# mLSTM attention and two MoE layers on one core: the last 64 input rows in another split, one pass for the weights' low part

## The chip, the core and the metric

The kernel runs on one core of one Trainium2 chip. The metric is the device time of one execution in microseconds (us), lower is better. TensorE (PE) multiplies 128x128 tiles, loads of its stationary operand (PEld) overlap with it; VectorE (DVE), ScalarE (ACT) and GpSimd (POOL) do elementwise work; SyncE (SP) issues every DMA. Each engine has its own queue of instructions, written out once, and works it off in order; semaphores order the engines among each other.

## The reference

```python
# attention: batch 2, 8 heads, 768 steps, head size 40
m_new = max(f + m, i);  f_stab = exp(f + m - m_new);  i_stab = exp(i - m_new)
C = f_stab * C + i_stab * outer(v, k);   n = f_stab * n + i_stab * k
y[t] = sigmoid(o) * (C @ q) / max(abs(n @ q), 1)
# x: (1536 tokens, 320), the heads side by side
def moe(x):   h = x @ w_in;  return (h - tanh(h)) @ w_out          # 320 -> 2048 -> 320
def moe2(x):  h = x @ w_in;  return (h * tanh(softplus(h))) @ w_out
out = moe2(moe(attention))                                        # weights are float64
```

## The kernel before

**Layout.** Tokens are cut into 12 pieces of 128: piece j holds chunk c = j // 2 of batch b = j % 2. Attention runs in chunks of 128 steps with a carried state `C`. Layer 0 (the first MoE) takes six blocks of two pieces, layer 1 three blocks of four. The 2048 hidden columns are 16 tiles f of 128; for each f the host lays the 128 columns of `w_in` (rows 0 to 127, 128 to 255, 320 columns of `w_out`, and the last 64 rows twice, one copy on each half of the partitions) side by side: 704 columns (`WC`) of float64, which arrive as pairs of 32-bit words.

**High and low parts.** TensorE multiplies a rounded float32 form. Each operand is kept as a high part (rounded by ACT) and a low part (the rest, from a subtraction), and a product is summed from high times high, high times low and low times high. `conv_w` makes a weight tile `w` from a `raw` tile: three passes over the raw words (L202 and L214 on DVE, L210 on ACT; for layer 1 also L204 on DVE, and L207 in place of L210), the high copy of 704 columns (L217, ACT), the low part of the first 576 columns (L220, DVE), and the low part of the upper 64 partitions of the last 128 columns, which overwrites the high part there (L221, DVE). For f = 0 of layer 0, L220 and L221 run on POOL. So the last weight piece (`PCH`) holds high over low.

`transpose_x` transposes a token piece by three PE transposes (`xt`, L288; the last 64 columns of x are doubled beforehand by a copy of ACT, L428), ACT copies the high part of all three pieces (L290) and DVE subtracts the low part of all three in one pass (L293). `mm1` (L576 on, matmul L586, tile `h`) does eight matmuls per f and block: HI0 and HI1 with x high, HI0 and HI1 with x low, LO0 and LO1 with x high, and `PCH` with the last x piece high and low.

**The rest of a tile.** `tile1` (L595 to L617) makes g from h on ACT (tanh twice, square, relu with bias) and DVE (two tensor operations, a predicated copy), ACT rounds it to `gh` (L597), POOL subtracts `gl` (L598); `mm2` (L649 to L651) multiplies by `w_out` into `acc`. `attention(j)` runs `nb` (PE, L358 from chunk 1 on), `Dm` (ACT exp, L361, then POOL's AFFINE_SELECT, L363), `dl` and `wv` (POOL), `sc` (PE) and DVE's product with `Dm` (L389), `it` and `pv` (PE), `hv`, `den` and `xo` (DVE, L401 to L423), then the transpose and the state update `st` (PE, L310).

**Order.** The program is recorded with attention, conversion of weights and layer 0 interleaved by tables of steps (`CUT`, `ahead`, `conv_to`), and a list scheduler that simulates durations sets the final order of each engine's queue. While the first eight weight tiles are converted, filler matmuls (`w_ps`, L690) stand in PE's queue. Between the tiles f = 4 to 7 of the first block, ACT loads another table, takes the sigmoid of the output gates for chunks 1 to 5 (L264) and loads the first table back.

**Slots.** Weight tiles have 16 slots, which the gate tiles (`n_all`, `n0`, `gi`, ...) hold first. The first four raw tiles lie in slots of the pool `xp` that later hold transposed x; the rest in three slots of `rawp`. `nr` (the gate rows that DMAs spread into `md` and `sd`) has a place of its own.

Of the kernel before, what the change touches and what calls it, by code (L numbers as in the profile page):

```python
# [8 lines left out]
F32 = mybir.dt.float32  # L9
F32R = mybir.dt.float32r  # L10
# [15 lines left out]
def kernel(  # L26
# [21 lines left out]
    REM0, REM1 = 256 + DM, 256 + DM + 128  # L48
    HI0, HI1, OUT_HI, PCH = 0, 128, 256, REM0
    LO0, LO1, OUT_LO = WC, WC + 128, WC + 256  # L50
    WT = WC + 256 + DM
# [64 lines left out]
    nr = once.tile([P, S - EC * L], F32R, name="nr")  # L116
# [57 lines left out]
    def load_w(n=1):  # L174
        for _ in range(n):
            if pending_loads:
                layer, f = pending_loads.pop(0)
                early = layer == 0 and f < ER
                t = (xp if early else rawp).tile(
                    [P, 2 * WC], U32, tag="x" if early else "raw", name="raw", bufs=NB - 1 if early else None  # L180
                )
                queued(
                    lambda: nc.sync.dma_start(out=t, in_=(w1, w2)[layer][f].bitcast(U32)), layer == 0 and f < CUT[0]
                )
                raw[layer, f] = t
# [3 lines left out]
    def conv_w(layer, f, first=(), behind=()):  # L189
# [29 lines left out]
        with after(scored[NP + 1] if (layer, f) == (0, CUT[0] - 1) else []):  # L219
            eng.tensor_tensor(w[:, WC:WT], in0=zf[:, 0:REM0], in1=wf[:, 0:REM0], op=ALU.subtract)  # L220
        lows[layer, f] = eng.tensor_tensor(w[64:P, REM0:REM1], in0=zf[64:P, REM0:REM1], in1=wf[64:P, REM0:REM1], op=ALU.subtract)  # L221
# [55 lines left out]
    def new_xT(layer, bi):  # L277
        nt = len(blk[layer, bi]) * L
        p, m = (late.get("x", xp), M1) if layer == 0 else (x2pool(bi), M2)
        t = p.tile([P, 2, 3, m], F32R, tag="x", name="xT", bufs=len(supers[0]) if layer else 1 if p is not xp else NB - 1)  # L280
        xT[layer, bi] = tuple(t[:, n, :, 0:nt] for n in range(2))

    def transpose_x(layer, bi, pos):
# [5 lines left out]
        hi, lo = (t[:, :, pos * L:(pos + 1) * L] for t in xT[layer, bi])  # L289
        chain[:] = [x, nc.scalar.activation(out=hi, in_=t_ps, func=AF.Copy)]  # L290

        def low():
            chain.append(nc.vector.tensor_tensor(lo, in0=t_ps, in1=hi.bitcast(F32), op=ALU.subtract))  # L293
# [281 lines left out]
    def mm1(i):  # L575
        l, bi, fs, nt = span(i)  # L576
        t = ps_h.tile([P, MX], F32, tag="h", name="h")[:, 0:len(fs) * nt]
        xh, xl = xT[l, bi]
        pairs = [
            (HI0, xh, 0), (HI1, xh, 1), (HI0, xl, 0), (HI1, xl, 1), (LO0, xh, 0), (LO1, xh, 1), (PCH, xh, 2), (PCH, xl, 2),  # L580
        ]
        for k, f in enumerate(fs):
            w = wtile[l, f]
            for n, (o, x, kk) in enumerate(pairs):
# [396 lines left out]
```

## Time and profile before

| what | value |
|---|---|
| median of 3 runs | 448.72 us (448.59 to 448.79) |
| the profiled execution | 447.9 us, of which its span 446.2 us |
| PE busy | 436.4 us (98%), 3114 matmuls |
| PEld busy | 399.5 us (90%) |
| DVE busy | 305.4 us (68%), 521 instructions |
| ACT busy | 283.5 us (64%), 519 instructions |
| POOL busy | 99.2 us (22%), 107 instructions |
| mean granted TensorE clock | 0.999 |

The span runs from the first to the last instruction; 1.7 us of the execution lie outside it. Matmuls are pipelined and each one's end is modelled, so PE's busy share counts time in which it is not at its peak, and the filler matmuls count as busy too. The share of DVE is a mean over stages: it is nearly full in the first 160 us and below a quarter in the last 86.

### The profile page before, as it was taken

Reading aid. Unit: us, or ns where it says so; the run is one execution under the profiler, and the core shown is the slowest. Engines: PE = TensorE matmul, PEld = TensorE weight load, DVE = VectorE, ACT = ScalarE, POOL = GpSimd, SP = SyncE. Lnnn points to the kernel's source line nnn. Section 1 sums busy time; section 2 is a strip of 40 time slices with the busy share of each in tenths; the row PEclk is TensorE's granted clock in tenths of the full one; section 3 lists DMA queues with packets and bytes.
Section 4 is the critical chain, followed back from the end, with each engine's and each line's share of the span. In section 5 each row is a group of like instructions: output and inputs, shape, how many; then the busy total and the mean of one; then the engine's idle time right before and its main releaser. Section 6 shows DMA issues by size and latency. Waiting matters only on the chain.

```text
span 446.2 us, 7979 instructions
## 1 busy us (share of the span) xinstructions
PE 436.4 (98%) x3114; PEld 399.5 (90%) x3114; DVE 305.4 (68%) x521; ACT 283.5 (64%) x519; POOL 99.2 (22%) x107
## 2 busy tenths in 40 slices
PE   9899989999999999999999999999999999999996
PEld 5657979899899999999999999999999888999996
DVE  7899999978899896578999987898522211211112
ACT  6687987485786858889889877666434322333331
POOL 2307235343452521333333331000000000000000
PEclk9999999999999999999999999999999999999999
DMA  8986526423244210002222110543010000100001
GB/s 247 368 301 206 187 62 226 125 70 95 62 151 136 66 67 0 1 2 66 65 67 66 65 66 0 195 132 128 0 60 0 1 1 1 42 18 0 1 0 59
DMA packets 22728, 38.03 MB, mean 85 GB/s; under 512 B 1348, under 2 KB 17028, under 8 KB 22692
## 3 DMA queue, kind: packets, MB, share of 16 engines
q1 hardware_dynamic: 22692, 37.54, 25.7%
q8 instruction: 24, 0.39, 0.4%
q14 instruction: 12, 0.10, 0.1%
HBM read 35.41 MB, written 1.97 MB: 84 GB/s over the span
## 4 chain that ended last, share of the span: by engine, by line
PE 86%; DVE 8%; ACT 4%; issue 1%; ACTq 0%; DVEq 0%
PE h L586 37%; PE acc L649 12%; PE acc L651 12%; PE acc L650 12%; PE pv L409 3%; PE sc L385 2%; PE w_ps L690 2%; PE it L396 2%; PE xt L288 2%; DVE g L613 1%; DVE t L614 1%; DVE g L617 1%; DVE Dm L389 1%; ACT raw L210 1%; PE nb L358 1%
## 5 line engine op out<-in xcount | busy, mean ns | idle before, releaser
L586 PE MATMUL h<-xT,w 128*128 128x256 f32 (+1 forms) x1152 | 205.8, 321 | 0.5 <-DVE w L220 0.2
L586 PEld LDWEIGHTS h<-xT,w 128*128 128x128 f32 x1152 | 168.7, 188 | 15.7 <-issue 0.9
L649 PE MATMUL acc<-w,gh 128*128 128x320 f32 x384 | 119.5, 312 | 0.6 <-ACT gh L597 0.4
L650 PE MATMUL acc<-w,gh 128*128 128x320 f32 x384 | 118.8, 310 | 0.0
L651 PE MATMUL acc<-w,gl 128*128 128x320 f32 x384 | 114.0, 310 | 0.0
L598 POOL TENSOR_TENSOR gl<-g,gh 128x512 fp32r<-128x512 f32 x48 | 62.5, 1303 | 139.1 <-ACT gh L597 134.1
L630 DVE TENSOR_TENSOR gl<-g,gh 128x512 fp32r<-128x512 f32 x48 | 33.2, 691 | 87.4 <-ACT g L629 87.2
L628 ACT ACTIVATE gh<-h 128x512 fp32r<-128x512 f32 x48 | 28.7, 598 | 78.1 <-PE h L586 78.0
L649 PEld LDWEIGHTS acc<-w,gh 128*128 128x128 f32 x384 | 72.2, 188 | 3.4 <-ACT gh L597 0.7
L650 PEld LDWEIGHTS acc<-w,gh 128*128 128x128 f32 x384 | 72.2, 188 | 2.4
L651 PEld LDWEIGHTS acc<-w,gl 128*128 128x128 f32 x384 | 70.4, 188 | 0.7 <-issue 0.4
L617 DVE COPY_PREDICATED g<-u,t 128x512 f32<-128x512 uint32 x48 | 39.3, 824 | 10.0 <-ACT u L615 9.6
L597 ACT ACTIVATE gh<-g 128x512 fp32r<-128x512 f32 x48 | 30.3, 632 | 22.8 <-DVE g L617 21.5
L613 DVE TENSOR_TENSOR g<-u,h 128x512 f32<-128x512 f32 x48 | 32.7, 680 | 13.8 <-ACT u L610 3.9
L615 ACT ACTIVATE u<-u,bias 128x512 f32<-128x512 f32 x48 | 34.8, 725 | 8.2 <-DVE g L613 8.2
L217 ACT ACTIVATE w<-raw 128x704 fp32r<-128x704 f32 x32 | 27.2, 861 | 10.8 <-DVE raw L214 10.5
L614 DVE TENSOR_TENSOR t<-h,t 128x512 f32<-128x512 f32 x48 | 32.8, 684 | 0.0
L214 DVE SCALAR_TENSOR_TENSOR raw<-raw 128x704 uint32<-128x704 uint32 x32 | 32.0, 1007 | 1.0 <-ACT raw L207 0.4
L220 DVE TENSOR_TENSOR w<-raw,w 128x576 fp32r<-128x576 f32 x31 | 29.1, 939 | 1.9 <-ACT w L217 1.8
L610 ACT ACTIVATE u<-u 128x512 f32<-128x512 f32 x48 | 30.4, 636 | 0.0
L608 ACT ACTIVATE u<-h 128x512 f32<-128x512 f32 x48 | 28.1, 585 | 1.3 <-PE h L586 1.3
L629 ACT ACTIVATE g<-h 128x512 f32<-128x512 f32 x48 | 28.5, 594 | 0.0
(108 smaller groups left out, 445.0 us busy)
## 6 DMA issues: line engine op xcount, KB each, us to landing
raw<-in_w_dram SPq DMA_DIRECT2D x32, 704.0 KB
qk_t<-in_qk_dram SPq DMA_DIRECT2D x12, 512.0 KB
kv_t<-in_kv_dram SPq DMA_DIRECT2D x12, 324.0 KB
out_dram<-xo SPq DMA_DIRECT2D x12, 160.0 KB
xo<-in_og_dram SPq DMA_DIRECT2D x2, 800.0 KB
xo<-in_og_dram SPq DMA_DIRECT2D x1, 320.0 KB
sd<-nr SPq DMA_DIRECT2D x20, 4.0 KB
md<-nr SPq DMA_DIRECT2D x10, 8.0 KB
```

The lines of the kernel that those rows point to most:

```text
L214: third[layer, f] = nc.vector.scalar_tensor_tensor(z, in0=z, scalar=3, in1=lo32, op0=ALU.logical_shift_left, op1=ALU.bitwise_or)
L586: y = nc.tensor.matmul(t[:, k * nt:(k + 1) * nt], lhsT=w[:, o:o + P], rhs=x[:, kk, :], start=(n == 0), stop=(n == len(pairs) - 1),)
L598: nc.gpsimd.tensor_tensor(gl, in0=g, in1=gh.bitcast(F32), op=ALU.subtract)
L610: squared[:] = [nc.scalar.activation(out=u, in_=u, func=AF.Square, scale=G_SA)]
L613: mark[:] = [nc.vector.tensor_tensor(g, in0=u, in1=h, op=ALU.mult)]
L614: nc.vector.tensor_tensor(t, in0=h, in1=t, op=ALU.subtract)
L615: relus[i] = nc.scalar.activation(out=u, in_=u, func=AF.Relu, bias=bias[:, 0:1])
L617: chosen[i] = nc.vector.copy_predicated(out=g, mask=u.bitcast(U32), data=t)
L630: mark.append(nc.vector.tensor_tensor(gl, in0=g, in1=gh.bitcast(F32), op=ALU.subtract))
L649: turn(lambda: nc.tensor.matmul(a, lhsT=gh[:, sl], rhs=wh, start=(f in ends_), stop=False))
L650: turn(lambda: nc.tensor.matmul(a, lhsT=gh[:, sl], rhs=wl, start=False, stop=False))
L651: turn(lambda: nc.tensor.matmul(a, lhsT=gl[:, sl], rhs=wh, start=False, stop=end))
```

## The change

The weight tile grows from 1280 to 1408 columns: both halves of the last piece keep the high part (`PCH`), and its low part lies behind the other low parts (`PCL`), on both halves. So one subtraction over 704 columns replaces the two passes of 576 and of 64x128. On the other side, the x tile has five pieces instead of six: pieces 0 to 2 are the high parts, where the upper half of piece 2 is overwritten by its low part (L292, 64x128), and pieces 3 and 4 are the low parts of the first two (L294, 128x256). `mm1` still does eight matmuls, in another order: the third is now `PCH` with piece 2, the last `PCL` with piece 2. The first four raw tiles now lie in slots of the weight tiles, and `nr` in a slot of `xp`.

```diff
--- before.py
+++ after.py
@@ -45,10 +45,9 @@
     NF, _, WC = w1.shape
     D1 = D + 1
     HP = P // 2
-    REM0, REM1 = 256 + DM, 256 + DM + 128
-    HI0, HI1, OUT_HI, PCH = 0, 128, 256, REM0
-    LO0, LO1, OUT_LO = WC, WC + 128, WC + 256
-    WT = WC + 256 + DM
+    HI0, HI1, OUT_HI, PCH = 0, 128, 256, 256 + DM
+    LO0, LO1, OUT_LO, PCL = WC, WC + 128, WC + 256, WC + 256 + DM
+    WT = 2 * WC
 
     BLOCKS = [2, 2, 2, 2, 2, 2]
     SUPER = [[4], [4], [4]]
@@ -113,7 +112,7 @@
     uT = once.tile([P, NCH, BH], F32, name="uT")
 
     EC = 1
-    nr = once.tile([P, S - EC * L], F32R, name="nr")
+    nr = xp.tile([P, S - EC * L], F32R, tag="x", name="nr", bufs=NB - 1)
 
 
 
@@ -176,9 +175,7 @@
             if pending_loads:
                 layer, f = pending_loads.pop(0)
                 early = layer == 0 and f < ER
-                t = (xp if early else rawp).tile(
-                    [P, 2 * WC], U32, tag="x" if early else "raw", name="raw", bufs=NB - 1 if early else None
-                )
+                t = (wp if early else rawp).tile([P, 2 * WC], U32, tag="w" if early else "raw", name="raw")
                 queued(
                     lambda: nc.sync.dma_start(out=t, in_=(w1, w2)[layer][f].bitcast(U32)), layer == 0 and f < CUT[0]
                 )
@@ -217,8 +214,7 @@
         cvd[:] = [nc.scalar.activation(out=w[:, 0:WC], in_=zf, func=AF.Copy)]
         eng = nc.gpsimd if (layer, f) == (0, 0) else nc.vector
         with after(scored[NP + 1] if (layer, f) == (0, CUT[0] - 1) else []):
-            eng.tensor_tensor(w[:, WC:WT], in0=zf[:, 0:REM0], in1=wf[:, 0:REM0], op=ALU.subtract)
-        lows[layer, f] = eng.tensor_tensor(w[64:P, REM0:REM1], in0=zf[64:P, REM0:REM1], in1=wf[64:P, REM0:REM1], op=ALU.subtract)
+            lows[layer, f] = eng.tensor_tensor(w[:, WC:WT], in0=zf, in1=wf[:, 0:WC], op=ALU.subtract)
         wtile[layer, f] = w
 
 
@@ -277,8 +273,10 @@
     def new_xT(layer, bi):
         nt = len(blk[layer, bi]) * L
         p, m = (late.get("x", xp), M1) if layer == 0 else (x2pool(bi), M2)
-        t = p.tile([P, 2, 3, m], F32R, tag="x", name="xT", bufs=len(supers[0]) if layer else 1 if p is not xp else NB - 1)
-        xT[layer, bi] = tuple(t[:, n, :, 0:nt] for n in range(2))
+        t = p.tile(
+            [P, 5 * m], F32R, tag="x", name="xT", bufs=len(supers[0]) if layer else 1 if p is not xp else NB - 1
+        )
+        xT[layer, bi] = t.rearrange("p (k t) -> p k t", k=5)[:, :, 0:nt]
 
     def transpose_x(layer, bi, pos):
         j = blk[layer, bi][pos]
@@ -286,11 +284,15 @@
         t_ps = at_ps([P, 3, P], "xt")
         for n in range(3):
             x = nc.tensor.transpose(t_ps[:, n, :], src[:, n * P:(n + 1) * P], ident)
-        hi, lo = (t[:, :, pos * L:(pos + 1) * L] for t in xT[layer, bi])
-        chain[:] = [x, nc.scalar.activation(out=hi, in_=t_ps, func=AF.Copy)]
+        t = xT[layer, bi][:, :, pos * L:(pos + 1) * L]
+        chain[:] = [x, nc.scalar.activation(out=t[:, 0:3], in_=t_ps, func=AF.Copy)]
 
         def low():
-            chain.append(nc.vector.tensor_tensor(lo, in0=t_ps, in1=hi.bitcast(F32), op=ALU.subtract))
+            y = t[64:P, 2]
+            nc.vector.tensor_tensor(y, in0=t_ps[64:P, 2], in1=y.bitcast(F32), op=ALU.subtract)
+            chain.append(
+                nc.vector.tensor_tensor(t[:, 3:5], in0=t_ps[:, 0:2], in1=t[:, 0:2].bitcast(F32), op=ALU.subtract)
+            )
 
         return low
 
@@ -575,13 +577,11 @@
     def mm1(i):
         l, bi, fs, nt = span(i)
         t = ps_h.tile([P, MX], F32, tag="h", name="h")[:, 0:len(fs) * nt]
-        xh, xl = xT[l, bi]
-        pairs = [
-            (HI0, xh, 0), (HI1, xh, 1), (HI0, xl, 0), (HI1, xl, 1), (LO0, xh, 0), (LO1, xh, 1), (PCH, xh, 2), (PCH, xl, 2),
-        ]
+        x = xT[l, bi]
+        pairs = [(HI0, 0), (HI1, 1), (PCH, 2), (HI0, 3), (HI1, 4), (LO0, 0), (LO1, 1), (PCL, 2)]
         for k, f in enumerate(fs):
             w = wtile[l, f]
-            for n, (o, x, kk) in enumerate(pairs):
+            for n, (o, kk) in enumerate(pairs):
                 with after([] if n else hold):
                     y = nc.tensor.matmul(
                         t[:, k * nt:(k + 1) * nt], lhsT=w[:, o:o + P], rhs=x[:, kk, :], start=(n == 0),
```

The number of instructions stays the same on PE (2862 in the program), ACT and SP. DVE loses 31 passes of 576 columns and 31 of 64x128 and gains 31 of 704; 24 passes of 3x128 become 24 of 64x128 and 24 of 2x128. POOL has one pass of 704 in place of its two. The scheduler also set the queues anew. Three places are shown; lines behind the first function are shifted by two.

**First block, attention of chunk 1.** PE's queue at the first `nb` of chunk 1, before:

```order
L586 MATMUL h<-xT,w 128x256 x4
L358 MATMUL nb<-md,sd_94 128x512
L358 MATMUL nb<-md,sd_95 128x512
L358 MATMUL nb<-md,sd_94 128x512
L586 MATMUL h<-xT,w 128x256 x2
L649 MATMUL acc<-w,gh 128x320
```

and now, behind the first five matmuls of f = 5 instead of the first four of f = 4:

```order
L586 MATMUL h<-xT,w 128x256 x5
L360 MATMUL nb<-md,sd_94 128x512
L360 MATMUL nb<-md,sd_95 128x512
L360 MATMUL nb<-md,sd_94 128x512
L586 MATMUL h<-xT,w 128x256 x3
```

Three of the four `nb` matmuls have moved to about the place where the fourth stood before: behind the rest of f = 4, twelve `acc` matmuls, two fillers and the first part of f = 5. POOL works on their results; before, from the `gl` of the first tile on:

```order
L598 TENSOR_TENSOR gl<-g,gh 128x512
L363 AFFINE_SELECT Dm<-Dm 128x512 x3
L167 TENSOR_SCALAR dl<-Dm 128x8
L363 AFFINE_SELECT Dm<-Dm 128x512
L373 TENSOR_TENSOR wv<-kv_t,dl 128x328
L167 TENSOR_SCALAR dl<-Dm 128x8
L373 TENSOR_TENSOR wv<-kv_t,dl 128x328
L598 TENSOR_TENSOR gl<-g,gh 128x512
```

and now:

```order
L598 TENSOR_TENSOR gl<-g,gh 128x512
L365 AFFINE_SELECT Dm<-Dm 128x512 x3
L166 TENSOR_SCALAR dl<-Dm 128x8
L375 TENSOR_TENSOR wv<-kv_t,dl 128x328
L598 TENSOR_TENSOR gl<-g,gh 128x512
L365 AFFINE_SELECT Dm<-Dm 128x512
```

The fourth AFFINE_SELECT (of the second piece of the chunk) has moved behind a `wv` and the `gl` of the second tile.

**First block, DVE at the last of the eight weight tiles.** Here `raw` in the SCALAR_TENSOR_TENSOR below the `Dm` rows is tile f = 7. Before:

```order
L202 TENSOR_SCALAR raw<-raw 128x704
L389 TENSOR_TENSOR Dm<-sc,Dm 128x512 x2
L214 SCALAR_TENSOR_TENSOR raw<-raw 128x704
L613 TENSOR_TENSOR g<-u,h 128x512
L614 TENSOR_TENSOR t<-h,t 128x512
L389 TENSOR_TENSOR Dm<-sc,Dm 128x512
L221 TENSOR_TENSOR w<-raw,w 64x128
L389 TENSOR_TENSOR Dm<-sc,Dm 128x512
L220 TENSOR_TENSOR w<-raw,w 128x576
```

and now (its first row is still tile f = 6):

```order
L211 SCALAR_TENSOR_TENSOR raw<-raw 128x704
L391 TENSOR_TENSOR Dm<-sc,Dm 128x512 x2
L217 TENSOR_TENSOR w<-raw,w 128x704
L199 TENSOR_SCALAR raw<-raw 128x704
L613 TENSOR_TENSOR g<-u,h 128x512
L614 TENSOR_TENSOR t<-h,t 128x512
L391 TENSOR_TENSOR Dm<-sc,Dm 128x512 x2
L211 SCALAR_TENSOR_TENSOR raw<-raw 128x704
```

The third raw pass of f = 7 stood behind the first pair of `Dm` products and now stands behind the second pair; the low part of f = 6 stands between the pairs.

**Second block, PE at the transposes of chunk 1.** Before:

```order
L288 MATMUL xt<-ident,xo 128x128 x3
L310 MATMUL st<-wv,kv_t 40x41 x8
L288 MATMUL xt<-ident,xo 128x128 x3
L310 MATMUL st<-wv,kv_t 40x41 x8
L586 MATMUL h<-xT,w 128x256 x6
L358 MATMUL nb<-md,sd_94 128x512
L358 MATMUL nb<-md,sd_95 128x512
L586 MATMUL h<-xT,w 128x256 x28
```

and now:

```order
L286 MATMUL xt<-ident,xo 128x128
L312 MATMUL st<-wv,kv_t 40x41 x8
L286 MATMUL xt<-ident,xo 128x128 x3
L312 MATMUL st<-wv,kv_t 40x41 x8
L586 MATMUL h<-xT,w 128x256 x6
L360 MATMUL nb<-md,sd_94 128x512
L586 MATMUL h<-xT,w 128x256 x3
L360 MATMUL nb<-md,sd_95 128x512
L586 MATMUL h<-xT,w 128x256 x26
```

Three `h` matmuls have moved in between the two `nb`. At the next chunk's transposes the queue moves too: before, 39 `acc` matmuls stood between the last `h` and the second piece's `xt`, now 43, and both `xt` groups with the `st` between them follow one another.

## Rows read from the trace of the kernel before

**Rows 1.** Busy time by stage: PE, PEld, DVE, ACT, POOL, clock, DMA.

```profile
20.00:60.00 40.00, 37.29 (x307) 28.72 (x308) 38.24 (x67) 33.56 (x58) 12.54 (x16) 1.00 0.70 224
...
91.00:446.00 355.00, 351.16 (x2427) 330.47 (x2427) 221.50 (x368) 213.92 (x395) 65.55 (x59) 1.00 0.16 53
```

**Rows 2.** Waits of PE: us in total, times, longest.

```profile
PE xt L288 <- DVE xo L423: 2.1, 3, 1.2
PE st L310 <- DVE xT L293: 1.4, 1, 1.4
```

**Rows 3.** DVE in order of time: start, us, line, operation.

```profile
19.22 0.55 DVE L293 TENSOR_TENSOR xT<-xt,xT 128x384 fp32r<-128x384 f32 x1
19.69 0.88 DVE L214 SCALAR_TENSOR_TENSOR raw<-raw 128x704 uint32<-128x704 uint32 x1
20.53 0.56 DVE L293 TENSOR_TENSOR xT<-xt,xT 128x384 fp32r<-128x384 f32 x1
...
21.87 0.75 DVE L220 TENSOR_TENSOR w<-raw,w 128x576 fp32r<-128x576 f32 x1
22.66 0.29 DVE L221 TENSOR_TENSOR w<-raw,w 64x128 fp32r<-64x128 f32 x1
22.98 0.81 DVE L525 TENSOR_TENSOR nr<-n_all,nr 16x640 fp32r<-16x640 f32 x1
...
42.50 1.28 DVE L389 TENSOR_TENSOR Dm<-sc,Dm 128x512 f32<-128x512 f32 x2
43.70 1.46 DVE L214 SCALAR_TENSOR_TENSOR raw<-raw 128x704 uint32<-128x704 uint32 x1
```

**Rows 4.** All engines at 17.5 us: POOL's first low pass, DVE beside it.

```profile
17.52 1.43 POOL L220 TENSOR_TENSOR w<-raw,w 128x576 fp32r<-128x576 f32 x1 [3.46 <-ACT w L217]
...
17.81 1.49 DVE L423 SCALAR_TENSOR_TENSOR xo<-xo,den 128x320 f32<-128x320 f32 x1
```

**Rows 5.** ACT in order of time around the sigmoids; idle time in brackets.

```profile
45.19 0.85 ACT L217 ACTIVATE w<-raw 128x704 fp32r<-128x704 f32 x1 [2.38 <-DVE raw L214]
46.06 1.28 ACT L264 ACT_TABLE_LOAD   x1
...
47.99 0.71 ACT L615 ACTIVATE u<-u,bias 128x512 f32<-128x512 f32 x1
...
49.76 0.63 ACT L597 ACTIVATE gh<-g 128x512 fp32r<-128x512 f32 x1 [0.43 <-DVE g L617]
```

**Rows 6.** POOL in order of time, attention of chunk 1.

```profile
36.68 2.75 POOL L363 TENSOR_SCALAR_AFFINE_SELECT Dm<-Dm 128x512 f32<-128x512 f32 x3 [1.05 <-ACT Dm L361]
39.52 0.56 POOL L167 TENSOR_SCALAR dl<-Dm 128x8 f32<-128x8 f32 x1
40.04 0.63 POOL L363 TENSOR_SCALAR_AFFINE_SELECT Dm<-Dm 128x512 f32<-128x512 f32 x1
40.65 1.23 POOL L373 TENSOR_TENSOR wv<-kv_t,dl 128x328 f32<-128x328 f32 x1
...
43.14 1.26 POOL L598 TENSOR_TENSOR gl<-g,gh 128x512 fp32r<-128x512 f32 x1
```

**Rows 7.** PE in order of time; idle time and its releaser in brackets.

```profile
34.18 0.86 PE L358 MATMUL nb<-md,sd 128*128 128x512 f32 x3
...
38.30 0.39 PE L358 MATMUL nb<-md,sd 128*128 128x512 f32 x1
...
57.31 0.51 PE L310 MATMUL st<-wv,kv_t 128*40 128x41 f32 x16 [1.37 <-DVE xT L293]
...
59.27 0.50 PE L358 MATMUL nb<-md,sd 128*128 128x512 f32 x1 [0.33 <-DVE xT L293]
59.60 3.43 PE L586 MATMUL h<-xT,w 128*128 128x256 f32 x28
...
84.17 0.41 PE L288 MATMUL xt<-ident,xo 128*128 128x128 f32 x2 [0.39 <-DVE xo L423]
...
87.60 0.41 PE L288 MATMUL xt<-ident,xo 128*128 128x128 f32 x2 [0.49 <-DVE xo L423]
```

## The prediction

> **What bounds the kernel now.** Read the busy times by stage first. From 91 us to the end PE is busy for 351.2 of 355 us [rows 1], one matmul behind the other, and the change leaves its matmuls alone: nothing done on DVE can shorten that stretch by more than the few tenths in which PE waits there. From 20 to 60 us DVE is busy for 38.2 of 40 us [rows 1] and PE for only 37.3, fillers counted. Then the view of what PE waited for: its two largest entries name DVE, 2.1 us in three waits for `xo` and 1.4 us in one wait for the low pass of the transposed x [rows 2]. Read last, the order of time shows where: 1.37 and 0.33 us at 57 and 59 us, 0.39 and 0.49 us at 84 and 87 us [rows 7]; the longest, 1.2 us, is at the start. So what can be won lies ahead of 91 us, and what counts is when PE gets past 59 us, and whether the two waits at 84 and 87 us stay.
>
> **The weights' low part.** Before, a weight's two passes take from 21.87 to 22.98 us, 1.11 us [rows 3]. The new pass reads two inputs of 704 columns, as the raw pass at 19.69 us does, which lets the next start after 0.84 us [rows 3]. I take -0.27 us a weight. With the durations alone (0.75 + 0.29 against 0.88) it would be -0.16; with the start of the small pass and of the one behind it, each 0.03 us after the end of the one ahead, where others start 0.04 to 0.08 us before it [rows 3], the larger value holds. Seven weights are done on DVE ahead of 48 us: -1.9 us of DVE work there; three more up to 73 us: -0.8. The other 21 lie where PE is full, and are worth nothing.
>
> The row shows the small pass starting 0.04 us after the pass ahead has ended and the next 0.03 us after it [rows 3]. The Trainium skill (VectorE: DVE Perf Modes, section "Two Vector instructions with no wait between them") gives a rule for that: an instruction whose operands start in another 32-partition quadrant than those of the instruction ahead starts only when all earlier ones are finished. The trace agrees. The rule speaks for the weights and against the x side: there the change adds a pass that starts at partition 64, twice held by that rule, 24 times. By that rule the dearer price of a transpose below holds, without it the cheaper one.
>
> **The transposed x.** One pass of 3x128 lets the next start after 0.47 us [rows 3]. Now a 64x128 pass comes first, then one of 2x128. For the first the nearest row is the small weight pass, 0.32 us from start to start, and 0.12 more for the lost overlap ahead; for the second, between 0.29 us (128 columns) and 0.55 us (384) [rows 3], 0.42 us of duration and 0.34 to the next start. Together 0.78, so +0.31 us a transpose; with no lost overlap at all 0.20 + 0.34, so +0.07. I take +0.31. Of the 24, four come ahead of 59 us; two of them right where PE waits.
>
> **POOL's first weight.** POOL's pass of 576 columns runs from 17.52 to 18.95 us, and DVE's `xo` beside it takes 1.49 us and ends 0.35 us after it [rows 4]. With 704 columns, scaled by columns, POOL ends at 19.26: +0.3 us for that `xo` and all behind it on DVE. It is hidden: the queue saves 0.27 us on the next weight, and 14 fillers stand in PE's queue before the next tile. Cost 0; if that cover fails, +0.3.
>
> The Trainium skill (SBUF — State Buffer, section "Who interferes with whom") says that the port pair that DVE shares with POOL is locked for a whole instruction. The 1.49 us agree; were it shared instead, the +0.3 would be about 0.
>
> **What the new order of the queues does, first block.** Here the seven weights' -1.9 us should show, and I think they don't, because ACT's queue decides. ACT converts f = 7 (45.19), loads the table at 46.06 and gets to the next work of the matmul chain only after the sigmoids and the second load [rows 5]. Its copy of f = 7 waits for DVE's third raw pass (43.70, 1.46 us) [rows 3], and that pass now stands behind the second pair of `Dm` products, and these behind the fourth AFFINE_SELECT on POOL. Step by step. The first `nb` were at 34.18; they now stand where the fourth did, at 38.30 [rows 7], less some 1 us that DVE has saved by then (four weights): 37.2. ACT's exp adds 0.7: 37.9. POOL's three AFFINE_SELECT take 2.75 us beside a busy DVE, 1.9 at the 0.63 us of the single one [rows 6]: 39.8 to 40.7. Then `dl` 0.56, `wv` 1.23, `gl` 1.26, AFFINE_SELECT 0.63 [rows 6]: 43.5 to 44.4. Two products 1.28, the raw pass 0.88 to 1.46 [rows 3]: 45.7 to 47.1, against 45.16 before. I take 46.4, so the table load comes 1.2 us later. ACT gives 1.05 of it back: `u` with bias (0.62 us to the next start) stood among the sigmoids and now stands ahead of the load, and the 0.43 us of idle time ahead of `gh` go [rows 5]. Left: +0.15 us, between -0.55 and +0.85.
>
> **Second block, 55 to 60 us.** `st` at 57.31 waits for the first low pass, now +0.31. The second `nb` at 59.27 waits for the second one, now +0.62; but three `h` matmuls stand in between, which PE does in that wait: 28 take 3.43 us [rows 7], so three take 0.37. Left +0.25.
>
> **At 84 and 87 us.** Four more `acc` matmuls, about 0.6 us (an estimate, by columns: an `h` matmul of 256 takes 0.122 us [rows 7], so one of 320 about 0.15), stand ahead of the second piece's transpose, and fourteen more ahead of the first. The wait of 0.39 us goes; of the 0.49 I take half, since DVE's chain shifts too: -0.6, between 0 and -0.9 [rows 7].
>
> **Slots and queues at no cost.** `nr` shares five slots with the x tiles, so block 4's x waits for the last DMAs out of `nr`. SP issues those once chunk 4's `nb` are done, with the rest of that chunk's attention still ahead of the transpose; a wait there would hold ACT's copy and all behind it. Weight tiles 4 to 15 take slots of gate tiles and of the first raw tiles, whose last readers stand ahead of them in the queues. Cost 0 each; SP's queue swaps only single DMAs.
>
> **Sum.** +0.15 + 0.25 - 0.6 = -0.2 us, on the profiled execution's 447.9, whose span is 446.2; it lies 0.8 below the median. On the median's scale: 448.5.
>
> **Rivals.** *DVE is the bound and the saving comes through (faster).* For it: DVE is full from 20 to 60 us. Then POOL is not late, the table load comes with DVE's gain, -1.9 + 0.62 = -1.3 us, the two x passes add 0.25 and the waits at 84 and 87 us go, -0.9: -1.9, so 446.8. If `u` moves out of the sigmoids on top, -2.5. Against it: ACT's chain through the tables.
>
> *POOL's fourth AFFINE_SELECT decides (slower).* One mechanism: on POOL it stands behind `wv` and `gl`, DVE's second `Dm` pair waits for it, the raw pass of f = 7 behind that, and ACT's table load behind that. It decides from the point at which that raw pass ends after 47.0 us. Price: +0.85 there, +0.25 at 59 us, and the waits at 84 and 87 us stay, since DVE is later too: +1.1 to +1.5, so 450.0. Against it: the gaps on POOL are not all needed, and AFFINE_SELECT alone takes 0.63.
>
> *The reordered queues behave otherwise further on.* PE's queue changes up to 180 us. The waits of PE there are few, so this is worth some tenths either way and only widens the range.
>
> **How the numbers follow.** What can be told from no change here is about 0.2%, 0.9 us: faster is under 447.8, slower over 449.6. My forecast, no change: 0.40, its own range 447.8 to 449.5. The saving comes through: 0.33. POOL decides: 0.27. The range has both other cases' centres in it and a little more: 446.3 (the faster one with `u` moved) to 450.6 (the slower one with +0.3 at the start and a wait kept).
>
> **What would show it.** Right: DVE's 704 pass at about 0.88 us, the next start at once; the 64x128 pass of x at 0.29; the first table load of the sigmoids at 47.0 to 47.5, with `u` ahead of it; `st` of block 1 waiting longer; no wait of PE for `xo` near 84 us. The total of DVE should fall by only 1 to 3 us. Wrong: a table load at or before 46 us, or the second `nb` of block 1 at or before 58.5 us, means that the saving came through; a raw pass of f = 7 that ends after 47 us means the slower case; a PE wait for a weight slot or for `nr` means that I took the slots too lightly.

## The result, and the profile after

| | before | after |
|---|---|---|
| median time, us | 448.69 | 451.52, ratio 1.006 (95%: 1.0039 to 1.0081) |
| a second series (a_again) | 448.63 | 451.36, ratio 1.0061 (1.0049 to 1.0073) |
| profiled execution, time and span, us | 447.9, 446.2 | 450.76, 449.0 |
| PE's first `pv` product to its last `acc` product, us | 12.14 to 442.48: 430.34 | 12.93 to 445.33: 432.40 |

The change costs 2.4 to 2.8 us; the time lies 0.5 to 0.9 above the predicted range. One of the six executions of the changed kernel took 613.96 us at a mean granted clock of 0.647; it counts in the median of 451.52 but not in the ratio, and the other five have a median of 451.08. The table's last line is needed because executions start differently. Up to the first `nb` the two kernels issue the same work, yet the 14 fill matmuls at the start took longer in the one execution than in the other. The first row of PE in order of time, then the first `pv` and the last `acc`, before and after (start, us, line, operation):

```profile
0.84 5.26 PE L690 MATMUL w_ps<-const-bfloat16-1.0 128*32 128x512 bf16 x14 [0.84 <-PEq L970]
...
12.14 1.98 PE L409 MATMUL pv<-kv_t,Dm 128*128 128x41 f32 x16
...
442.48 0.30 PE L651 MATMUL acc<-w,gl 128*128 128x320 f32 x1
```

```profile
0.84 6.06 PE L690 MATMUL w_ps<-const-bfloat16-1.0 128*32 128x512 bf16 x14 [0.84 <-PEq L970]
...
12.93 1.31 PE L411 MATMUL pv<-kv_t,Dm 128*128 128x41 f32 x10
...
445.33 0.30 PE L651 MATMUL acc<-w,gl 128*128 128x320 f32 x1
```

Over all profiles of this study they take 4.57 to 6.06 us. So 0.79 of the 2.8 us between the two spans belong to the execution. Below, "+n" is a time counted from the profile's own first `pv` product. 2.06 us are left to explain.

The single passes cost about what was worked out. DVE in order of time, after (against [rows 3] and [rows 4]), and POOL's first low pass:

```profile
18.61 1.78 DVE L425 SCALAR_TENSOR_TENSOR xo<-xo,den 128x320 f32<-128x320 f32 x1
...
21.07 0.88 DVE L211 SCALAR_TENSOR_TENSOR raw<-raw 128x704 uint32<-128x704 uint32 x1
21.98 0.29 DVE L292 TENSOR_TENSOR xT<-xt,xT 64x128 fp32r<-64x128 f32 x1
22.31 0.42 DVE L294 TENSOR_TENSOR xT<-xt,xT 128x256 fp32r<-128x256 f32 x1
22.65 0.52 DVE L199 TENSOR_SCALAR raw<-raw 128x704 uint32<-128x704 uint32 x1
...
29.81 1.68 DVE L217 TENSOR_TENSOR w<-raw,w 128x704 fp32r<-128x704 f32 x2
```

```profile
18.33 1.71 POOL L217 TENSOR_TENSOR w<-raw,w 128x704 fp32r<-128x704 f32 x1 [3.48 <-ACT w L214]
```

The pair of weight passes, each of 0.88 us, takes 1.68 us together, so the second starts 0.80 us behind the first. The two x passes take 0.33 and 0.34 us from start to start, and the first of them starts 0.91 us behind the raw pass ahead of it. `xo` beside POOL's pass takes 1.78 us. What was not worked out is the first block's eighth weight, f = 7. DVE in order of time (against the last rows of [rows 3]):

```profile
42.63 1.29 DVE L391 TENSOR_TENSOR Dm<-sc,Dm 128x512 f32<-128x512 f32 x2 [2.50 <-PE sc L387]
44.00 1.28 DVE L217 TENSOR_TENSOR w<-raw,w 128x704 fp32r<-128x704 f32 x1
45.21 0.95 DVE L199 TENSOR_SCALAR raw<-raw 128x704 uint32<-128x704 uint32 x1
46.08 0.67 DVE L613 TENSOR_TENSOR g<-u,h 128x512 f32<-128x512 f32 x1
46.67 0.68 DVE L614 TENSOR_TENSOR t<-h,t 128x512 f32<-128x512 f32 x1
47.28 1.27 DVE L391 TENSOR_TENSOR Dm<-sc,Dm 128x512 f32<-128x512 f32 x2
48.47 0.88 DVE L211 SCALAR_TENSOR_TENSOR raw<-raw 128x704 uint32<-128x704 uint32 x1
```

POOL in the same stretch (against [rows 6]), and ACT (against [rows 5]):

```profile
40.36 1.81 POOL L365 TENSOR_SCALAR_AFFINE_SELECT Dm<-Dm 128x512 f32<-128x512 f32 x3 [4.85 <-ACT Dm L363]
...
43.24 1.29 POOL L598 TENSOR_TENSOR gl<-g,gh 128x512 fp32r<-128x512 f32 x1
44.48 1.29 POOL L365 TENSOR_SCALAR_AFFINE_SELECT Dm<-Dm 128x512 f32<-128x512 f32 x1
```

```profile
46.79 0.73 ACT L615 ACTIVATE u<-u,bias 128x512 f32<-128x512 f32 x1 [1.54 <-DVE g L613]
49.38 0.86 ACT L214 ACTIVATE w<-raw 128x704 fp32r<-128x704 f32 x1 [1.87 <-DVE raw L211]
50.27 1.28 ACT L260 ACT_TABLE_LOAD   x1
...
55.33 1.28 ACT L741 ACT_TABLE_LOAD   x1
```

The raw pass ends at 49.35 (+36.42) against 45.16 (+33.02): 3.40 later. POOL's mask ended at 45.77, but the second `Dm` pair starts at 47.28, with no idle time ahead of it: DVE was busy with four other passes. The raw pass is late because of where it stands in DVE's queue, not because DVE waits for the mask. DVE did wait earlier, 2.50 us for `sc` ahead of the first `Dm` pair, which is behind the late `nb` in PE's queue. That pair starts at +29.70 against +30.36, so most of the time that DVE had saved by then went into this wait, and all that stands behind it gained only 0.66 us. The table load follows the raw pass (+37.34 against +33.92). Then PE ahead of the second block (against [rows 7]), and the stretches behind (busy time of PE, PEld, DVE, ACT, POOL, then granted clock, DMA):

```profile
57.03 0.33 PE L286 MATMUL xt<-ident,xo 128*128 128x128 f32 x1 [0.66 <-ACT xo L162]
...
58.66 0.33 PE L286 MATMUL xt<-ident,xo 128*128 128x128 f32 x1 [0.49 <-ACT xo L162]
60.70 0.51 PE L312 MATMUL st<-wv,kv_t 128*40 128x41 f32 x16 [1.70 <-DVE xT L294]
61.14 1.51 PE L586 MATMUL h<-xT,w 128*128 128x256 f32 x6
```

```profile
60.00:62.00 2.00, 1.30 (x20) 1.28 (x21) 1.89 (x6) 0.32 (x1) 0.00 (x0) 0.83 0.05 18
62.00:64.00 2.00, 2.00 (x10) 1.81 (x9) 1.97 (x4) 2.00 (x3) 1.29 (x1) 0.50 0.59 166
64.00:66.00 2.00, 2.00 (x16) 2.00 (x15) 1.94 (x4) 1.89 (x4) 0.82 (x2) 0.82 0.00 0
```

PE stands idle for 0.66, 0.49 and 1.70 us, and behind that the granted clock is at 0.50, which is 1.2 GHz, for part of three stretches: 0.34 + 1.00 + 0.36 = 1.7 us of full-speed work lost. Six `h` matmuls take 1.31 us to the next start there, against 0.73 at the 0.122 us of [rows 7]. In the profile of before the clock stays at 1.00 from 58 to 66 us; one of its stretches:

```profile
62.00:64.00 2.00, 2.00 (x17) 1.96 (x17) 1.95 (x2) 2.00 (x5) 1.86 (x2) 1.00 0.03 8
```

Last, what PE waited for (us, times, longest; against [rows 2]):

```profile
PE st L312 <- DVE xT L294: 1.7, 1, 1.7
PE xt L286 <- DVE xo L425: 1.5, 1, 1.5
PE xt L286 <- ACT xo L162: 1.2, 2, 0.7
```

Of the three waits for `xo` on DVE the one at the start is left; those at 84 and 87 us are gone. No wait of PE names a weight slot or `nr`.

### The profile page after: what moved, and what is told of

Its sections match the earlier page's. It is cut to its first block, busy times and chain, and to the rows that moved or that the text cites. A ratio compares the mean times of both kernels' runs of the same rounds, so it can differ in the third digit from the quotient of the medians.

```text
span 449.0 us, 7978 instructions
## 1 busy us (share of the span) xinstructions
PE 438.6 (98%) x3114; PEld 400.9 (89%) x3114; DVE 298.4 (66%) x514; ACT 284.2 (63%) x519; POOL 100.5 (22%) x106
## 4 chain that ended last, share of the span: by engine, by line
PE 88%; DVE 7%; ACT 3%; issue 1%; DVEq 0%
PE h L586 39%; PE acc L649 12%; PE acc L651 12%; PE acc L650 12%; PE pv L411 3%; PE sc L387 2%; PE it L398 2%; PE w_ps L690 1%; PE xt L286 1%; DVE raw L211 1%; DVE w L217 1%; DVE raw L199 1%; PE nb L360 1%; ACT xo L260 1%; DVE xo L425 1%
## 5 line engine op out<-in xcount | busy, mean ns | idle before, releaser
L586 PE MATMUL h<-xT,w 128*128 128x256 f32 (+1 forms) x1152 | 207.9, 322 | 0.9 <-DVE w L217 0.4
L586 PEld LDWEIGHTS h<-xT,w 128*128 128x128 f32 x1152 | 170.7, 190 | 17.1 <-DVE xT L292 0.9
L598 POOL TENSOR_TENSOR gl<-g,gh 128x512 fp32r<-128x512 f32 x48 | 64.7, 1348 | 128.8 <-ACT gh L597 128.8
L597 ACT ACTIVATE gh<-g 128x512 fp32r<-128x512 f32 x48 | 30.3, 632 | 18.4 <-DVE g L617 17.3
L217 DVE TENSOR_TENSOR w<-raw,w 128x704 fp32r<-128x704 f32 x31 | 33.4, 1085 | 1.7 <-ACT w L214 1.6
L211 DVE SCALAR_TENSOR_TENSOR raw<-raw 128x704 uint32<-128x704 uint32 x32 | 30.7, 962 | 0.8 <-ACT raw L204 0.2
L609 ACT ACTIVATE t<-h 128x512 f32<-128x512 f32 x48 | 28.6, 596 | 0.0
```

What stands on the lines that cost most here:

```text
L211: third[layer, f] = nc.vector.scalar_tensor_tensor(z, in0=z, scalar=3, in1=lo32, op0=ALU.logical_shift_left, op1=ALU.bitwise_or)
L217: lows[layer, f] = eng.tensor_tensor(w[:, WC:WT], in0=zf, in1=wf[:, 0:WC], op=ALU.subtract)
L586: y = nc.tensor.matmul(t[:, k * nt:(k + 1) * nt], lhsT=w[:, o:o + P], rhs=x[:, kk, :], start=(n == 0), stop=(n == len(pairs) - 1),)
L598: nc.gpsimd.tensor_tensor(gl, in0=g, in1=gh.bitcast(F32), op=ALU.subtract)
```

## Experiments

Theory: the change's order of the first block (late `nb`, and f = 7's raw pass behind the second `Dm` pair) makes PE late and idle, and the clock falls on top. Rivals: the new passes' own work costs it; or the late mask alone does.

| profile | table load | second `st` | first `pv` to last `acc`, us | granted clock below 1.00 at | median time, us |
|---|---|---|---|---|---|
| before | +33.92 | +45.17 | 430.34 | none of 20 to 70 us | 448.4 to 448.8 in five series |
| b_nblate | +33.87 | +45.04 | 430.96 | 58 to 64 | 448.46 |
| b_sttlate | +36.01 | +46.04 | 432.70 | 60 to 66 | 450.39 |
| b_fill | +34.00 | +45.23 | 430.43 | none | 448.76 |
| bs_fill | +36.07 | +46.11 | 432.27 | none | 450.52 |
| after | +37.34 | +47.77 | 432.40 | 60 to 66 | 451.52 |
| a_again | +38.54 | +48.96 | 434.47 | 22 to 26, 58 to 68 | 451.36 |
| a_fill | +37.32 | +47.75 | 431.55 | none | 449.34 |
| stt_first | +37.43 | +47.86 | 431.58 | 20 to 26 | 449.15 |
| s_fill2 | +36.09 | +46.52 | 430.21 | none | 448.09 |

The runs were made in several series, each with the kernel before beside it; its medians differ by 0.4 us, so times of different series compare no better than that.

A late table load by itself is not a late end: bs_fill and s_fill2 load the table at the same time and end 2.06 us apart.

**The same kernel again.**

> The changed kernel itself, once more. Two parts of the loss are to be seen again or not. Launch theory: of the 2.8 us between the two profiled spans 0.8 us arose before any changed instruction ran, since the first 14 fill matmuls took 6.06 us and not 5.26; if that differs between executions of one program, they take anything from 5.2 to 6.1 here, and all that follows starts by as much earlier or later. Order theory (the first block's last weight chunk comes late, PE stands idle ahead of the second block and its clock falls): second table load at 49.5 to 50.4 us, the longest wait of PE ahead of the second block 1.5 to 1.8 us, granted clock near 0.5 to 0.8 somewhere between 60 and 66 us; time 450.5 to 452, ratio to before 1.004 to 1.008.

Here the 14 fill matmuls took 5.27 us, so the launch theory holds. This profile has a second fall, behind the wait for the second `xt` (1.54 us):

```profile
22.00:24.00 2.00, 2.00 (x7) 1.31 (x8) 1.97 (x3) 1.99 (x5) 0.00 (x0) 0.54 0.95 343
24.00:26.00 2.00, 2.00 (x10) 1.22 (x8) 1.94 (x5) 1.51 (x4) 0.00 (x0) 0.61 1.04 404
```

From +37.34 to +38.54, that fall moves the table load by 1.2 us (to 50.69, above the range expected). In the two series, four of the other eleven executions of the changed kernel have a mean clock of 0.996 (450.56 to 451.48 us), four of 0.991 (450.65 to 451.54) and three of 0.989 (451.97 to 452.91); none of them reaches the 0.999 or 1.000 that profiles without a fall show.

**The late `nb` alone, in the kernel before.**

```diff
             if i == 1:
+                mm2(qm.pop(0))
+                accl[:] = turned[-1:]
                 ahead(4)
...
-                nc.tensor.matmul(flat, lhsT=sds[b], rhs=md_[:, hf]...)
+                with after(accl):
+                    nc.tensor.matmul(flat, lhsT=sds[b], rhs=md_[:, hf]...)
```

> The kernel before, all its arithmetic as it was, with PE's three nb products of the first block pinned behind the first tile's acc products, as they stand in the changed kernel; POOL's fourth mask falls behind the 512-wide low pass by it, as there, but on VectorE the eighth chunk's last raw pass stays ahead of the second pair of Dm products. If the late nb and mask alone are enough: table load 2 to 3 us later than 46.06, time 449.7 to 451, ratio 1.002 to 1.005. If what decides is the raw pass's place behind the second pair on VectorE: table load by 47.2, no fall of the clock, 448.3 to 449.3, ratio 0.999 to 1.001.

448.46 us, ratio 0.9994 (0.9982 to 1.0006). POOL's mask now stands behind `gl`, as in the changed kernel, and DVE's raw pass keeps its place ahead of the second pair:

```profile
41.85 1.57 POOL L600 TENSOR_TENSOR gl<-g,gh 128x512 fp32r<-128x512 f32 x1
43.37 0.64 POOL L365 TENSOR_SCALAR_AFFINE_SELECT Dm<-Dm 128x512 f32<-128x512 f32 x1
```

```profile
43.40 1.36 DVE L215 SCALAR_TENSOR_TENSOR raw<-raw 128x704 uint32<-128x704 uint32 x1
```

So neither the late `nb` nor the late mask costs anything.

**And the raw pass behind the second pair, in the kernel before.**

```diff
-        with after(behind):
+        with after(scored[NP + 1] if (layer, f) == (0, CUT[0] - 1) else behind):
             third[layer, f] = ...
```

> The kernel before, all its arithmetic as it was, with the three nb products late (as in b_nblate, which cost nothing) and now also the eighth chunk's last raw pass pinned behind the second pair of Dm products on VectorE, which is the changed kernel's order. If that place is what costs (raw pass behind a pair that waits for POOL's fourth mask): the raw pass ends near 48, the table load starts near 48.7 and not 45.7, the second states product comes near 59 and not 56.9, time 450 to 451.5, ratio 1.003 to 1.006, without any of the change's arithmetic. If the changed arithmetic is needed for the loss: 448.2 to 449, ratio 0.999 to 1.001.

450.39 us, ratio 1.003 (1.0018 to 1.0041), with none of the change's arithmetic. DVE and ACT in order of time:

```profile
45.38 1.28 DVE L391 TENSOR_TENSOR Dm<-sc,Dm 128x512 f32<-128x512 f32 x2
46.58 1.18 DVE L215 SCALAR_TENSOR_TENSOR raw<-raw 128x704 uint32<-128x704 uint32 x1
```

```profile
48.68 1.28 ACT L265 ACT_TABLE_LOAD   x1
```

The table load is 2.1 us later than in b_nblate, so the place of one pass in DVE's queue makes the larger part of the loss here. It is not quite the changed kernel's queue: only two passes stand between the pairs, not four, and the raw pass ends at +35.09, not +36.42.

**The raw pass put back ahead, in the changed kernel.**

```diff
-        with after(scored[NP + 1] if (layer, f) == (0, CUT[0] - 1) else []):
+        with after(scored.get(NP + 1, []) if (layer, f) == (0, CUT[0] - 1) else []):
             lows[layer, f] = ...
...
+            with after([third[0, CUT[0] - 1]] if j == NP + 1 else []):
                 scored.setdefault(j, []).append(...)
...
-                lead1(min(CUT[0], f + PRE + NP), start)
+                lead1(min(CUT[0], f + PRE + NP + 2 * (i == 1)), start)
```

> The changed kernel with one thing of its order put back: the last raw pass of the first block's eighth weight chunk stands on VectorE ahead of the second pair of Dm products (and POOL's fourth mask ahead of the 512-wide low pass). All arithmetic of the change stays. Order theory: that raw pass ends at about 46.5 us and not 49.35, the table load starts near 47.3 and not 50.3, the first states product of the second block near 58 and not 60.7, the clock doesn't fall behind it; time 448.4 to 449.4, ratio 0.999 to 1.002. Rival, the work itself (the second pass of every xT, the wider low pass, POOL's wider pass) costs it: 450.5 to 452 as before, whatever the order.

449.15 us, ratio 1.0025 (1.0002 to 1.0048). Most of the loss is gone with all of the change's arithmetic in place, which speaks against the rival of the work itself. POOL's fourth mask goes back ahead of `gl` with it; that the late mask costs nothing was shown in the old order only (b_nblate). But the table load of this profile is no earlier (+37.43), because the clock fell at 20 to 26 us; against a_again, which has that fall too, it is 1.1 us earlier. Nine of 12 executions have a mean clock of 0.996 (448.25 to 449.75 us), three of 0.988 or 0.989 (451.67 to 453.0).

**Fill matmuls against the falls.** First with 11 of them around the second block, as `keep(n, x)` behind its transposes:

> The changed kernel with its order of the first block as it is, and 11 fill matmuls (0.235 us each) put into PE's waits ahead of the second block (two behind the second transpose of each tile, seven ahead of the second states product). Clock theory: the raw pass, the table load (50.3) and the second states product (60.7) come as late as in the changed kernel, but the granted clock stays at 1.00 from 58 to 66 us, and the 1.6 us that matmuls at the lower level cost there are saved: 449 to 450.2, ratio 1.001 to 1.003. Rival, lateness alone: the clock's fall cost little, since the work behind had slack: 450.5 to 452.

452.73 us, ratio 1.0092 (1.0079 to 1.0105), with the clock at 1.00. It tells nothing of the clock: the fills also changed the order behind 60 us, and PE then waits 0.73 us at 72 and 0.95 us at 92 us on DVE, where the changed kernel has no wait. With five in each wait the rest of the order stays:

```diff
-        keep(4, chain[0])
+        keep(9, chain[0])
...
             x = nc.tensor.transpose(t_ps[:, n, :], src[:, n * P:(n + 1) * P], ident)
+            if (layer, bi, pos, n) == (0, 1, 1, 2):
+                keep(5, x)
```

> The changed kernel with five more fill matmuls in PE's wait for the second xt (18 to 20 us) and five in its wait ahead of the second states product (59 to 61 us); the order of everything else stays as in the changed kernel, except that one nb product stands one acc product earlier. Clock theory: the granted clock is 1.00 in every stretch of 2 us from 16 to 70 us in most executions (mean clock 0.999 or 1.000 and not 0.989 to 0.996), and 0.8 to 1.6 us come back: 449.6 to 450.6, ratio 1.002 to 1.0045. Order theory without the clock: the table load still starts near 50, PE is as late, and what the clock cost is regained by slack behind: 450.5 to 452.

449.34 us, ratio 1.0011 (1.0002 to 1.002), every execution at a mean clock of 0.999 or 1.000. PE and the stretches (as above):

```profile
59.89 0.51 PE L314 MATMUL st<-wv,kv_t 128*40 128x41 f32 x16 [0.51 <-DVE xT L296]
```

```profile
60.00:62.00 2.00, 2.00 (x27) 1.62 (x26) 1.91 (x5) 0.79 (x2) 0.08 (x1) 1.00 0.24 51
62.00:64.00 2.00, 2.00 (x17) 1.95 (x17) 2.00 (x3) 2.00 (x3) 1.50 (x1) 1.00 0.31 115
```

The second `st` comes as late as in the changed kernel (+47.75 against +47.77), and still some 2 us come back, more than expected: that is what the falls cost by the medians. Between the two profiles it is 0.85 us; the profiled execution of after has one fall, and the table's a_again has two. Once more, for a second profile:

> The kernel of a_fill once more for a second profile: launch fill matmuls anything from 4.9 to 6.1 us, granted clock 1.00 from 16 to 70 us, time 448.4 to 450.

448.75 us, and 431.58 from the first `pv` to the last `acc`, as in a_fill. Then each wait filled alone:

> The changed kernel with the five fill matmuls at 18 to 20 us alone; order of all else as in the changed kernel. If the clock's falls at 22 to 26 us, behind the wait for the second xt, are the costlier ones (a_again: 1.2 us): mean clock up to 0.996 in most executions, 450.2 to 450.8, and none above 451.5. If those at 60 to 66 us are: 450.8 to 451.6, mean clock 0.991.

> The changed kernel with the five fill matmuls ahead of the second block's second states product alone. If the falls at 60 to 66 us cost (after: 0.85 us between its first pv product and its last acc product, against a_fill): 449.8 to 450.8, mean clock 0.996 in most executions, the rest being the falls at 22 to 26 us. If they cost nothing: 451 to 451.7.

450.78 us (1.0041; 1.0029 to 1.0053) and 449.66 us (1.003; 1.0018 to 1.0043). Filling the wait at the start gains some 0.7 us, filling the one ahead of the second `st` some 1.8, so the falls at 60 to 66 us cost most. With only the second wait filled, five of nine executions have no fall at all, so the longer wait at the start is not always followed by one.

**The yardsticks with the clock held.** The kernel before with the same fills (five, and four ahead of the second `st`), in its own order and in that of b_sttlate:

> The kernel before with fill matmuls in the same two waits as in a_fill (five more at 18 to 20 us, four ahead of the second states product); its order is unchanged otherwise. It gives the yardstick with the clock held. Clock theory with slack: falls of the clock cost the kernel before little, because PE waits for the second and third xo at 84 to 88 us anyway (0.4 and 0.5 us): 448.1 to 448.7, ratio 0.998 to 1.000, mean clock 0.999 or 1.000 in nearly all executions. If falls cost it as much as they cost the changed kernel: 447 to 447.8.

> The kernel before in the changed kernel's order (late nb, eighth chunk's raw pass behind the second pair of Dm products, as in b_sttlate) with the fill matmuls of b_fill. If the order's lateness, with the clock held, is what is left of the loss in a_fill (449.34): 449 to 449.6 here as well, ratio 1.0005 to 1.002. If the changed arithmetic (second xT pass, wider passes) is what is left: 448.2 to 448.7 here.

448.76 us (1.0006; 0.9994 to 1.0017) and 450.52 us (1.0042; 1.003 to 1.0054). Fills bring the kernel before nothing. The order costs 1.8 us with the clock held, more than expected. And a_fill, with the late raw pass too but with the rest of the change (its arithmetic, and PE's new order up to 91 us), is 1.2 us faster than bs_fill, 1.6 with each less the kernel before of its own series. At the second `st` a_fill is 1.64 us behind bs_fill and at the last `acc` 0.72 ahead, so it makes up 2.36 us between. Part of that shows on PE, bs_fill and then a_fill:

```profile
86.31 0.41 PE L289 MATMUL xt<-ident,xo 128*128 128x128 f32 x2 [0.80 <-DVE xo L427]
...
89.74 0.41 PE L289 MATMUL xt<-ident,xo 128*128 128x128 f32 x2 [0.49 <-DVE xo L427]
```

```profile
88.31 0.49 PE L286 MATMUL xt<-ident,xo 128*128 128x128 f32 x3
89.48 0.55 PE L286 MATMUL xt<-ident,xo 128*128 128x128 f32 x3
```

Two waits for `xo`, 1.29 us, are gone with the change; where the other 1.1 us come from was not found. To see whether the low part does it, the weights' low part in two passes again:

```diff
-            lows[layer, f] = eng.tensor_tensor(w[:, WC:WT], in0=zf, ...)
+            eng.tensor_tensor(w[:, WC:PCL], in0=zf[:, 0:PCH], ...)
+        lows[layer, f] = eng.tensor_tensor(w[:, PCL:WT], in0=zf[:, PCH:WC], ...)
```

> The kernel of a_fill (changed kernel, both waits filled, clock held) with the weights' low part again in two passes, 576 and 128 columns, on POOL for the first weight and on VectorE for the others; result as with one pass. With the clock held the changed arithmetic in the late order was 1.2 us faster than the old arithmetic in it (449.34 against 450.52). If the one-pass low part is what gives that: 450.2 to 450.7, the table load some 0.5 to 1.5 us later than in a_fill (37.3 us after the first pv product there). If it is not: 449.2 to 449.7, the table load within 0.3 us.

450.09 us (1.0046; 1.0024 to 1.0069); the seven executions at a mean clock of 0.999 or 1.000 have a median of 449.78, 0.4 above a_fill, and the two spreads overlap (449.49 to 450.23 against 448.37 to 449.97). The expectations are not clearly told apart: about a third of the 1.2 us may be the one-pass low part (its order behind the second block differs too), and the rest is open. The profile is one with long falls (mean 0.981), so its table load says nothing.

**The change, its raw pass ahead, and fills.** First at the start only:

> The changed kernel with the raw pass put back ahead of the second pair of Dm products (as in stt_first), and five more fill matmuls in PE's wait for the second xt at 18 to 20 us; the order of all else is that of stt_first. In stt_first the clock fell at 22 to 26 us behind that wait and the first h tile took 1.5 us longer. Clock theory: no fall there, table load at 47.5 to 48.5 and not 49.35, time 447.8 to 448.8, ratio 0.998 to 1.000, and few executions near 452. Rival, the start's lateness is taken up by slack behind: 448.7 to 449.5 as stt_first, ratio 1.001 to 1.003.

451.67 us (1.0032; 1.0009 to 1.0056), in two groups: five executions at 0.996 with 448.63 to 449.21 us, six at 0.988 or 0.989 with 451.61 to 452.16, one at 455.99. The start was held, but as in stt_first PE waits for the second `Dm` pair, and behind it lies a fall of some 10 us (a_fill_2p has one as long, from 15 to 25 us):

```profile
48.85 1.42 PE L412 MATMUL pv<-kv_t,Dm 128*128 128x41 f32 x11 [0.79 <-DVE Dm L392]
```

```profile
50.00:52.00 2.00, 2.00 (x15) 2.00 (x15) 1.97 (x6) 1.99 (x4) 0.00 (x0) 0.70 0.26 76
52.00:56.00 4.00, 4.00 (x21) 4.00 (x20) 1.66 (x5) 3.78 (x7) 2.17 (x3) 0.50 0.67 218
56.00:60.00 4.00, 4.00 (x18) 4.00 (x18) 2.47 (x8) 1.75 (x4) 0.00 (x0) 0.50 0.31 93
```

Then with that wait filled too (three behind the `it` products of the third attention tile, `keep(3, y)`, and five ahead of the second `st`), in two series:

> The changed kernel with the raw pass ahead of the second pair of Dm products (stt_first) and fill matmuls in all three of its waits: five more at 18 to 20 us, three ahead of the first pv products at 48 us (where s_fill lost the clock for 10 us behind a wait of 0.8 us), five ahead of the second states product. Clock theory: no executions near 452, mean clock 0.999 or 1.000, time 447.8 to 448.7, ratio 0.998 to 1.000: at least as fast as before. Rival: the change's own work keeps it 0.3 to 0.6 us behind b_fill.

> The kernel of s_fill2 once more, to learn whether it is faster than the kernel before: 447.8 to 448.4, ratio 0.997 to 0.9995, mean clock 0.999 in nearly all executions.

448.09 us in both; ratios 0.9985 (0.997 to 1.000) and 0.9986 (0.9977 to 0.9995), no execution above 448.8. This version beats the kernel before by 0.3 and 0.7 us by the medians (by the ratio clear of 1 in the second series only), the kernel before with fills (b_fill, same series as the first) by 0.7, and the changed one by 3.3. `nb` stands late in it too, and DVE waits 2.48 us for `sc`; so these two alone don't make it slower than the kernel before.

## Why the prediction was wrong

The 2.06 us between the two profiles can be split in two ways, each step from one kernel of the table to the next. By way of the old arithmetic: +0.09 for fills (b_fill), +1.84 for the order (bs_fill), -0.72 for the rest of the change in it (a_fill), +0.85 for one fall of the clock (after). By the median times, each less the kernel before of its own series, the last three are +1.8, -1.6 and +1.9 to +2.2. By way of the changed kernel: -0.13 for all of it with its raw pass ahead and fills (s_fill2), +1.34 for the raw pass behind (a_fill), +0.85 for the fall (after). Either way the loss is the order and the fall.

- **Weights' low part, -0.27 each:** right, if a little low (0.80 against 1.11 us from start to start in the pair at 29.81). Of its worth ahead of 48 us nothing was seen at the table load, as forecast, but not for the reason given: ACT's queue didn't hide it, DVE's wait of 2.50 us for `sc` took it up. Some of it may show at 86 to 90 us.
- **Transposed x, +0.31 each:** right. Both passes take 0.67 us against 0.47, +0.20, and the overlap lost ahead of them comes on top: 0.91 us from the raw pass to the first x pass, against 0.84 in [rows 3], so +0.27. The wait of the second `st` grew by 0.33 (1.70 against 1.37).
- **POOL's first weight, cost 0:** the size was right, +0.28 on POOL and +0.29 on `xo`, the cover was not there. The `xo` ends 0.35 us behind POOL's pass in both profiles, as [rows 4] had it. The Trainium skill (SBUF — State Buffer, section "Who interferes with whom") calls the port pair that the two engines share an exclusive lock, and these rows agree. PE's wait for the second `xt` went from 1.25 to 1.54 us and the eight `h` products behind it take 1.84 us to the next start (21.73 to 23.57) against 1.40 (20.65 to 22.05), since they wait for both low passes of the second x; so the 14 fills that were to hide it start 0.72 us later (+13.20 against +12.48).
- **New order, first block, +0.15: the step that failed.** Its chain followed POOL to the fourth mask and took DVE to be free behind it ("two products 1.28, the raw pass 0.88 to 1.46"). Two terms of it were off. The smaller is the late `nb`: "less some 1 us that DVE has saved by then" did not reach PE. The first `nb` came at +26.33, where the fourth had been at +26.16, and POOL began its masks at +27.43, which is 39.6 on the clock of before and not 37.9. POOL then worked faster than assumed, and the fourth mask ended at 45.0 on that clock, 0.6 us above the range. The larger is DVE's own queue, which holds four passes between the two pairs (1.28, 0.95, 0.67, 0.68), 3.3 us from start to start. So the second pair started 1.5 us after the mask had ended, and the raw pass ended 3.4 us later than before and not 1.2. By the prediction's own sign (a raw pass that ends after 47 us) this is its slower rival, which had the right chain from the raw pass on and a wrong cause ahead of it. Of the 3.4 us, 1.2 are the place behind the second pair: in s_fill2, with the raw pass ahead of that pair, it ends at +35.19. What ACT gives back was right: 1.15 us (second table load +42.40 against +40.13, 2.27 later) where 1.05 was taken.
- **Second block, +0.25:** about right in size (the wait of `st` grew by 0.33, and with the clock held, in a_fill, the second `nb` follows `st` after 2.06 us against 1.96) but for what it starts from; `st` comes 2.60 us later.
- **At 84 and 87 us, -0.6:** right in kind: both waits gone, 0.9 us. In bs_fill, with PE's old order there, they stay.
- **Slots and queues, 0:** right; no wait of PE names them.
- **Missing: the clock.** The sum had PE's idle time as a delay only. The changed kernel's three waits (0.66, 0.49, 1.70) are followed by a fall in the profile of after, and in that of a_fillhead, where the start is held; the mean clock of all five executions of a_fillhead (0.991 or 0.996) agrees. The fall is the 0.85 us above, and some 2 us by the medians.
- **"DVE's total falls by 1 to 3 us":** it fell by 7.0 (305.4 to 298.4): weights 39.9 to 33.4, x 13.3 to 17.3, which is 2.5; the other 4.5 are in the remaining passes, `den` (a TENSOR_TENSOR of eight columns, 5.9 to 2.2) above all.

Which part of the change turned the order stays open. With the low part in two passes again (a_fill_2p) `nb` still stands behind five `h` matmuls; no run has the other parts alone.

## What to carry to other kernels

Follow a moved instruction on its own engine's queue first and count every pass between its old and its new place; only then ask what it waits for. Read the mean clock of each execution beside its time: a wait of PE costs its own length and, where a fall follows, more on top (some 3 us between the two groups of s_fill, behind a wait of 0.8), unless later waits give it back. A late pass is not yet a late end: ask where PE waits behind it anyway. Where a wait can't be avoided, a few fill matmuls in it are cheap, but see that they don't turn the order behind them.

## What the hardware showed beyond expectation

Falls of TensorE's clock to a granted 0.50, 1.2 GHz, came behind single waits of 0.8 to 1.7 us between busy stretches, and not in every execution: the wait of 0.8 us ahead of `pv` had no fall behind it in stt_first and one of some 10 us in s_fill. They show as steps in the mean clock. For the kernel before, over four series, 37 executions at 0.998 or more have a median of 448.36 us, 49 at 0.996 of 448.79 and four at 0.985 of 451.64: one fall costs it 0.4 us, most likely since it waits for `xo` at 84 and 87 us anyway.

The start varies by itself: 14 fill matmuls of 512 columns, the same in every kernel, take 4.57 to 6.06 us, because the step from 0.43 us a matmul (512 columns, so 1.2 in a ns) to 0.22 comes earlier or later, behind the 7th in s_fill2, the 10th in before and not at all within the 14 in after; the granted clock reads 1.00 there all the same, so it doesn't show this. So does the end: b_fill's last product starts at 442.52 us, as in before (442.48), but its span is 2.2 us longer.
